# A Fourier filter layer with a two-layer network behind it: other load times in the opening, other PSUM banks for two pieces, and another order of the turned array

## The chip, the cores and the metric

The kernel runs on one core of one Trainium2 chip. A core has a tensor engine (PE, with weight loads shown as PEld), a vector engine (DVE), a scalar engine (ACT), GpSimd (POOL) and SyncE (SP); here POOL and SP mostly issue DMAs, which 16 DMA engines carry out. The metric is the device time of one execution in microseconds (us). The kernel before takes 773.05 us, the median of three runs (772.27 to 773.88).

## What is computed

Eight sequences of 3008 tokens with 256 channels are filtered in the frequency domain, and each token then goes through a two-layer network with a PReLU:

```python
X = np.fft.rfft(x, axis=1)                    # x: (8, 3008, 256)
Y = X * (filt_r + 1j * filt_i)[None]          # (1505, 256)
y = np.fft.irfft(Y, n=3008, axis=1).reshape(24064, 256)
h = y @ w_in                                  # (256, 2048)
g = np.maximum(h, 0) + alpha * np.minimum(h, 0)
out = g @ w_out                               # (2048, 256)
```

## The kernel before

**The whole.** The transform of length 3008 = 94 x 32 is made by matmuls: a first stage over 94 (piece_a), a second over 32 (piece_b) with the product with the filter, the inverse second stage (piece_c), and the inverse first stage (half_d, pair_d), whose result yT has the channels on the partitions and is kept in fp16. The network takes yT in blocks of 512 (or 384) tokens: `up` multiplies by w_in, ACT copies PSUM to gtb, DVE applies the slope, `down` multiplies by w_out, ACT copies out, SP stores. The schedule is written by hand: a plan says at which of 768 steps of the network each piece of the later sequences' transforms is issued, so that PE always has network matmuls to do. Each engine runs its own instructions in program order and waits on semaphores for the others.

**The opening.** The first sequence (class `First`) has nothing to hide behind, so its transform is written out by hand, with matmuls on an identity (`warm`, L438) that keep PE running where it would wait:

- Eight pieces of the first stage (L328), fed by eight DMAs of x from POOL. Piece i writes two PSUM banks (f = 0, 1) and is evicted into `am` (a view of gtb) by ACT or DVE in turn; for pieces 6 and 7 ACT takes f = 0 and DVE f = 1.
- The forward table twf comes in three DMAs from SP (L417), 8 of 24 columns each. The second and third are held back by a small DVE memset of their target (L445 behind piece 3, L453 behind piece 5). From each part PE and ACT make a part of the inverse table (`inverse_table`, L421), and `swapped` (L428, L429) makes from it, by scalings on DVE (part 0) or POOL (parts 8 and 16), a second table twx with swapped signs.
- The filter comes in three groups of eight DMAs from POOL (L140). The second half of the last group is issued behind the scalings of part 8.
- `turn_at` (L343) turns `am` by matmuls with the identity into `at`; `piece_b` (L355) multiplies by the table; DVE multiplies by the filter (L360); `piece_c` (L382) makes the inverse second stage from `uu` with the tables twi and twx as moving operands, into two `op` banks for two successive pieces; `keep_c` evicts these into `vm` (the tile v). There are twelve piece_b and twelve piece_c, kp = 0 to 11.
- `turn` (L399) turns `vm` back, 96 columns at a time, into zt: 32 values of s, two halves f of the channels, so 64 loads of weights. `half_t` does two s in one bank, `piece_t` four in two banks; piece_t(4) to piece_t(7) stand in the plan at steps 19 to 34.
- `half_d` multiplies zt by the inverse table wi3. half_d(0) (channels 0 to 127) and half_d(2) (channels 128 to 255) each need s = 0 to 3, that is half_t(0) and half_t(1).
- The first block goes through `up4` (L569): for each of four columns blocks h the two halves kt of the channels one after the other.

Within `vm` a value stands at (g, q, k, e), where s = 4g + e, q is one of four rows of the inverse table (parity and real or imaginary) and k one of 24 frequencies. So the 96 columns of one s that L399 loads are 4 elements (8 bytes) apart. L382 reads its table for that as

```python
tw, tx = (t.rearrange("p k (c g e) -> p k g c e", c=2, e=4) for t in (twi_s, twx_s))
```

which is runs of four elements, and writes runs of eight. The rows of wi3 have the order (q, k), as in the other sequences.

SP issues the constants that are needed later (wi3, al16, id32, wf1, wfq; L471 to L477) behind the tables. POOL loads the weights w_in and w_out and the next x (L484 to L491) in the loop over kp, behind a DVE memset of win_s (L482) at kp = 4.

Of the kernel before, what the change touches and what calls it, by code (L numbers as in the profile page):

```python
# [14 lines left out]
N1 = 94  # L15
# [10 lines left out]
def _build_consts():  # L26

    n1, n2, p = np.arange(N1), np.arange(N2), np.arange(32)
    k1 = (2 * (np.arange(NK) // 2) + 24 * (np.arange(NK) % 2))[None, :] + np.arange(2)[:, None]
    k2 = np.where(p < 16, p, 47 - p)  # L30
    g = np.where(p < 16, 1.0, -1.0)

    a1 = 2 * np.pi * n1[:, None, None] * k1[None] / N1
    wf1 = np.stack([np.cos(a1), -np.sin(a1)], axis=2)
    scale = np.where((k1 == 0) | (k1 == 47), 1.0, 2.0)[None, :, None, :] / NFFT
    wi3 = (wf1 * scale).reshape(N1, 96).T
    wfx = wf1.transpose(0, 3, 1, 2).reshape(N1, 96)
    wfq = np.zeros((2, 64, 64))
    wfq[:, :47, :48] = wf1[:47].transpose(1, 0, 2, 3).reshape(2, 47, 48)
    wfq = wfq.reshape(128, 64)  # L40
    wf1 = wf1.reshape(N1, 96)

    kk = k1[:, :, None] + N1 * k2
    ang = 2 * np.pi * n2[:, None, None, None] * kk[None] / NFFT
    c, s = np.cos(ang), np.sin(ang)
    fwd = np.array([[c, -s * g], [s, c * g]])
    twf = fwd.transpose(3, 0, 2, 4, 1, 5).reshape(128, NK, 64)
    return wf1, wfx, wfq, wi3, twf


@with_exitstack
def kernel(
# [8 lines left out]
    out: bass.AP,  # L61
):
    nc = tc.nc
    names = ("wf1", "wfx", "wfq", "wi3", "twf")
    consts = {n: nc.inline_tensor(np.ascontiguousarray(v).astype(np.float16), name="c_" + n)
              for n, v in zip(names, _build_consts())}
    signs = [np.tile(np.repeat([1.0, -1.0], r), 64 // r) for r in (16, 32)]
# [19 lines left out]
    wfq_s = konst.tile([128, 64], FP16, name="wfq_s")  # L87
    wfx_s = konst.tile([N1, 96], FP16, name="wfx_s")
    wi3_s = konst.tile([96, N1], FP16, name="wi3_s")
    twf_s = konst.tile([128, NK, 64], FP16, name="twf_s")  # L90
    twi_s = konst.tile([128, NK, 64], FP16, name="twi_s")
    filt_s = konst.tile([128, 12, 2, D], FP16, name="filt_s")
# [66 lines left out]
    class Fft:  # L159
        def __init__(self, b):  # L160
            self.b = b
            self.base = (b % 2) * NFFT
            self.uw = {}

        def start_a(self):
# [114 lines left out]
        def inverse(self, pd, g, dh, mh):  # L280
            ps = pd[:, 0 : 4 * N1].rearrange("p (m x) -> p m x", m=4)
            for m in range(4):
                nc.tensor.matmul(ps[:, m], self.zt[:, 8 * g + 4 * mh + m, dh * 128 : dh * 128 + 128],  # L283
                                 wi3_s, start=True, stop=True)
            return ps

        def half_d(self, i, evict, kind, fill=0):
# [25 lines left out]
    class First(Fft):  # L313
# [7 lines left out]

        def piece_a(self, i, wide):
            c, sh = i // 2, i % 2
            ps = banks(wide)
            for f in range(2):
                for u in range(4):
                    o = (4 * sh + u) * D + 128 * f
                    nc.tensor.matmul(ps[:, f, 96 * u : 96 * u + 96], xc[(0, c)][0:N1, o : o + 128], wfx_s,  # L328
                                     start=True, stop=True)
            o = self.am.rearrange("p (f m s) -> p f m s", f=2, s=N2)[:, :, :, 4 * i : 4 * i + 4]  # L330
            s = ps[:, :, 0:384].rearrange("p f (s m) -> p f m s", s=4)
            if i < 6:
                both[i % 2](o, s)
            else:
                for f in range(2):
                    both[f](o[:, f], s[:, f])

        def turn_at(self, kp, n, evict, wide=False):
            ps = banks(wide)
# [23 lines left out]
        def piece_c(self, kp):  # L363
            if kp % 2 == 0 and kp < 10:
                self.ops = [psO.tile([128, 2, D], FP32, name="op") for _ in range(2)]
            if kp == 10:
                pf = banks(False)
                self.ops = [pf[:, e].rearrange("p (k d) -> p k d", k=2) for e in range(2)]
            if kp == 11:
                pf = [bank(kind) for kind in ("h", "o")]  # L370
                self.ops = [t.rearrange("p (k d) -> p k d", k=2) for t in pf]
            kb = 0 if kp > 9 else kp % 2
            u = self.uw.pop(kp)
            tw, tx = (t.rearrange("p k (c g e) -> p k g c e", c=2, e=4) for t in (twi_s, twx_s))
            for par in range(2):
                for f in range(2):
                    for i, t in enumerate((tw, tx)):
                        for e in range(2):
                            r = slice(64 * e, 64 * e + 64)
                            o = self.ops[e][:, kb].rearrange("p (g w) -> p g w", g=16)  # L380
                            o = o[:, 8 * f : 8 * f + 8, 8 * par : 8 * par + 8]
                            nc.tensor.matmul(o.rearrange("p g (c e) -> p g c e", c=2),  # L382
                                             u[r, par, i, 128 * f : 128 * f + 128], t[r, 2 * kp + par],
                                             start=(i == 0), stop=(i == 1))

        def keep_c(self, kp, evicts, n=2):
            vm = self.vm.rearrange("p (g q k e) -> p g q k e", q=4, k=NK, e=4)
            for e in range(2):
                k = 2 * kp + e
                evicts[e](vm[:, :, :, k : k + 2 * n - 1 : 2],  # L390
                          self.ops[e][:, 0:n].rearrange("p k (g q e) -> p g q k e", q=4, e=4))

        def turn(self, pt, i, n):
            m = self.vm.rearrange("p (g m e) -> p g m e", m=96, e=4)
            for u in range(n):
                for f in range(2):
                    o = 256 * (u % 2) + 128 * f
                    s = n * i + u
                    nc.tensor.matmul(pt[0:96, u // 2, o : o + 128], m[:, 8 * f + s // 4, :, s % 4], id16,  # L399
                                     start=True, stop=True)  # L400

        def half_t(self, i, kind):
            pt = bank(kind).unsqueeze(1)
# [12 lines left out]
    def table(ka, kb):  # L416
        nc.sync.dma_start(out=twf_s[:, ka:kb], in_=consts["twf"].ap()[:, ka:kb])  # L417
# [24 lines left out]
    for i in range(8):  # L442
        f0.piece_a(i, i % 3 < 2)
        if i == 3:
            nc.vector.memset(twf_s[:, 8:16, 0:1], 0.0)  # L445
            table(8, 16)
            inverse_table(0, bank("o"))
            swapped(0, nc.vector)
            warm(3, bank("o"))
        elif i % 2 == 1:  # L450
            warm((8, 0, 6, 0)[i // 2], bank("o"))
        if i == 5:
            nc.vector.memset(twf_s[:, 16:24, 0:1], 0.0)  # L453
            table(16, 24)
    load_filt(nc.gpsimd, filt_s, 4, 8)
    warm(5, bank("o"))
    f0.turn_at(0, 1, on_act)
# [2 lines left out]
    f0.piece_b(0)  # L460
    f0.turn_at(2, 2, on_act)
    inverse_table(8, bank("o"))
    load_filt(nc.gpsimd, filt_s, 8, 12, (0,))
    swapped(8, nc.gpsimd)
    load_filt(nc.gpsimd, filt_s, 8, 12, (1,))
    f0.piece_b(1)
    inverse_table(16, bank("o"))
    swapped(16, nc.gpsimd)
    f0.piece_b(2)
    f0.turn_at(4, 2, on_act)  # L470
    nc.sync.dma_start(out=wi3_s, in_=consts["wi3"].ap())  # L471
# [4 lines left out]
    for r in (slice(0, 64), slice(64, 128)):  # L476
        nc.sync.dma_start(out=wfq_s[r], in_=consts["wfq"].ap()[r])  # L477
    for kp in range(12):
        if 0 < kp < 10:
            f0.piece_b(kp + 2)  # L480
        if kp == 4:
            nc.vector.memset(win_s[:, :, 0:1], 0.0)  # L482
            for kt in range(2):
                nc.gpsimd.dma_start(out=win_s[:, kt], in_=moe_w_in[kt * 128 : (kt + 1) * 128])  # L484
            xc[(1, 0)] = load_x(1, 0)
            for q in range(2):
                nc.gpsimd.dma_start(
                    out=wout_s[:, 8 * q : 8 * q + 8],
                    in_=moe_w_out[1024 * q : 1024 * q + 1024].rearrange("(j p) d -> p j d", p=128))
            for c in range(1, 4):  # L490
                xc[(1, c)] = load_x(1, c)  # L491
# [12 lines left out]
    for o in (32, 96):  # L504
        nc.gpsimd.dma_start(out=filt_s[o : o + 32], in_=filt_s[o - 32 : o])
    warm(3, bank("h"))
    on_dve(*f0.half_t(0, "o"))
    on_act(*f0.half_t(1, "o"))
    later = [f0.half_t(2, "h"), f0.half_t(3, "f")]
    f0.half_d(0, on_act, "o")  # L510
    f0.half_d(2, on_dve, "o")

    sizes = [512] * 5 + [384] + [512] * 6
    blocks = []
# [21 lines left out]
    class Block:  # L536
# [26 lines left out]
        def up4(self, i, half, mid):  # L563
            ps = psH.tile([128, 2, 512], FP32, name="hps").rearrange("p b (q c) -> p (b q) c", q=2)
            t = slice(256 * half, 256 * half + 256)
            for h in range(4):
                j = 4 * i + h
                for kt in range(2):
                    nc.tensor.matmul(ps[:, h], win_s[:, kt, j * 128 : (j + 1) * 128], yT[:, kt, t],  # L569
                                     start=(kt == 0), stop=(kt == 1))  # L570
            for fn in mid:
                fn()
            if half == 0:
# [190 lines left out]
```

## Time and profile before

| what | value |
|---|---|
| median of three runs | 773.05 us (772.27 to 773.88) |
| the profiled execution | 772.3 us, span 770.5 us, granted clock 1.0 |
| PE busy | 760.9 us, 99% of the span |
| weight loads (PEld) busy | 510.2 us, 66% |
| DVE busy | 634.2 us, 82% |
| ACT busy | 583.2 us, 76% |
| POOL busy | 147.9 us, 19% |
| 64 weight loads of L399 | 182 ns mean |
| 192 matmuls of L382 | 186 to 200 ns each, overlapping |
| 12 multiplications of L360 | 1215 ns each |

The span is the time from the first to the last record of the profiled execution; the execution's own time is 1.8 us longer. Matmuls overlap in the record, so the distance from one start to the next says more than a duration. In the timeline and the chain a row is start, time, engine, line, operation, out<-in, and behind a bracket the idle time before it with what ended it. A line with L is a line of the kernel before, except where the changed kernel is named.

### The profile page before, as it was taken

Reading aid. Unit: us, or ns where it says so; the run is one execution under the profiler, and the core shown is the slowest. Engines: PE = TensorE matmul, PEld = TensorE weight load, DVE = VectorE, ACT = ScalarE, POOL = GpSimd, SP = SyncE. Lnnn points to the kernel's source line nnn. Section 1 sums busy time; section 2 is a strip of 40 time slices with the busy share of each in tenths; the row PEclk is TensorE's granted clock in tenths of the full one; section 3 lists DMA queues with packets and bytes.
Section 4 is the critical chain, followed back from the end, with each engine's and each line's share of the span. In section 5 each row is a group of like instructions: output and inputs, shape, how many; then the busy total and the mean of one; then the engine's idle time right before and its main releaser. Section 6 shows DMA issues by size and latency. Waiting matters only on the chain.

```text
span 770.5 us, 16598 instructions
## 1 busy us (share of the span) xinstructions
PE 760.9 (99%) x6550; PEld 510.2 (66%) x6550; DVE 634.2 (82%) x1160; ACT 583.2 (76%) x671; POOL 147.9 (19%) x278
## 2 busy tenths in 40 slices
PE   8999999999999999999999999999999999999998
PEld 4666657666666666666666666766666666766666
DVE  4888885889889998899988998999877888666663
ACT  4787788888778787887778777787767777776663
POOL 7620560132211212121201222022101212000000
PEclk9999999999999999999999999999999999999999
DMA  9995797664954558633883538644473223510111
GB/s 162 148 239 156 134 208 195 171 164 119 200 138 94 138 126 169 185 83 94 188 213 89 124 98 177 182 99 117 119 160 98 68 72 96 152 36 28 42 42 56
DMA packets 96814, 99.77 MB, mean 129 GB/s; under 512 B 12020, under 2 KB 83076, under 8 KB 96544
## 3 DMA queue, kind: packets, MB, share of 16 engines
q1 hardware_dynamic: 82048, 69.22, 32.7%
q0 software_dynamic: 14688, 29.49, 21.4%
q8 instruction: 51, 0.84, 0.5%
q14 instruction: 27, 0.22, 0.1%
HBM read 54.74 MB, written 46.66 MB: 132 GB/s over the span
## 4 chain that ended last, share of the span: by engine, by line
PE 96%; ACT 3%; issue 0%; DVE 0%; DMA 0%; ACTq 0%
PE op L600 42%; PE hps L546 41%; PE psF L283 3%; PE hps L261 2%; PE psF L230 1%; PE hps L176 1%; PE op L438 1%; PE hps L202 1%; ACT asb L305 1%; PE hps L569 1%; ACT v L305 1%; PE op L382 1%; PE psF L399 0%; ACT gtb L577 0%; ACT gtb L555 0%; PE hps L355 0%
## 5 line engine op out<-in xcount | busy, mean ns | idle before, releaser
L555 ACT ACTIVATE gtb<-hps 128x1024 f16<-128x1024 f32 (+1 forms) x376 | 377.4, 1006 | 134.7 <-PE hps L546 131.6
L600 PE MATMUL op<-wout_s,gtb 128*128 128x256 f16 x3008 | 431.4, 273 | 0.0
L546 PE MATMUL hps<-yT,win_s 128*128 128x512 f16 (+1 forms) x1504 | 418.4, 375 | 0.9 <-ACT asb L305 0.5
L600 PEld LDWEIGHTS <-gtb 128*128 128x128 f16 x3008 | 290.8, 98 | 164.5 <-issue 11.0
L558 DVE TENSOR_SCALAR m<-gtb,alm_s 128x512 f16<-128x512 f16 (+1 forms) x752 | 227.2, 346 | 98.4 <-ACT gtb L555 96.9
L560 DVE TENSOR_TENSOR gtb<-gtb,m 128x2048 f16<-128x2048 f16 (+1 forms) x188 | 226.1, 1203 | 10.7 <-DVE m L558 0.5
L546 PEld LDWEIGHTS <-win_s 128*128 128x128 f16 x1504 | 142.5, 98 | 55.2 <-issue 6.6
L244 POOL DMA_DIRECT2D sw<-ww x144 | 71.6, 505 | 414.6 <-DVE ww L237 408.8
L605 ACT ACTIVATE osb<-op 128x512 f32<-128x512 f32 (+1 forms) x97 | 56.6, 584 | 12.6 <-PE op L600 11.5
L305 ACT ACTIVATE asb<-hps 128x1024 f16<-128x1024 f32 (+1 forms) x56 | 56.6, 1020 | 5.6 <-PE hps L176 4.3
L305 ACT ACTIVATE v<-hps 128x1024 f16<-128x1024 f32 (+1 forms) x43 | 43.4, 1010 | 10.8 <-PE hps L261 10.6
L237 DVE TENSOR_TENSOR ww<-psF,filts_s 128x1024 f16<-128x1024 f32 x42 | 51.1, 1218 | 0.2 <-PE psF L230 0.2
L238 DVE TENSOR_TENSOR uu<-psF,filt_s 128x1024 f16<-128x1024 f32 x42 | 51.0, 1214 | 0.0
L305 ACT ACTIVATE yT<-psF 128x752 f16<-128x752 f32 x58 | 46.1, 796 | 2.0 <-PE psF L283 1.9
L283 PEld LDWEIGHTS <-zt 96*128 96x128 f16 x512 | 28.6, 98 | 6.3 <-issue 0.6
L283 PE MATMUL psF<-wi_s,zt 96*128 96x94 f16 x496 | 31.0, 205 | 0.3 <-DVE yT L308 0.2
L249 DVE TENSOR_TENSOR uu<-uu,sw 128x1024 f16<-128x1024 f16 x36 | 24.6, 683 | 1.7 <-DMA sw<-ww 1.3
L242 POOL DMA_DIRECT2D uu<-ww x24 | 19.5, 1238 | 33.0 <-DVE uu L238 24.9
L118 POOL DMA_DIRECT2D xs<-in_x_dram x32 | 21.6, 889 | 13.0 <-PE hps L546 4.9
L186 DVE TENSOR_TENSOR xs<-xs 47x2048 f16<-47x2048 f16 x16 | 19.5, 1220 | 0.4
L190 DVE TENSOR_TENSOR xs<-xs 47x2048 f16<-47x2048 f16 x16 | 19.3, 1209 | 0.0
L261 PE MATMUL hps<-uu,twi_s 64*64 64x256 f16 x336 | 17.3, 281 | 0.0
(86 smaller groups left out, 264.2 us busy)
## 6 DMA issues: line engine op xcount, KB each, us to landing
out_dram<-osb SPq DMA_DIRECT2D x128, 128.0 KB
v_dram<-v SPq DMA_DIRECT2D x84, 128.0 KB
zt<-v_dram SPq DMA_DIRECT2D x28, 384.0 KB
sw<-ww POOLq DMA_DIRECT2D x144, 64.0 KB, 2.8
xs<-in_x_dram POOLq DMA_DIRECT2D x44, 192.0 KB, 6.3
at<-a_dram SPq DMA_DIRECT2D x40, 192.0 KB
a_dram<-asb SPq DMA_DIRECT2D x32, 192.0 KB
a_dram<-asb SPq DMA_DIRECT2D x12, 384.0 KB
```

The lines of the kernel that those rows point to most:

```text
L237: nc.vector.tensor_mul(ww, px, fs)
L238: nc.vector.tensor_mul(uu, px, f)
L244: nc.gpsimd.dma_start(out=sw[o : o + 32], in_=ww[i : i + 32])
L261: nc.tensor.matmul(ps[64 * par : 64 * par + 64, e, 256 * h : 256 * h + 256], twi_s[r, 4 * q + 2 * h + par], u[r, par, h], start=True, stop ...
L283: nc.tensor.matmul(ps[:, m], self.zt[:, 8 * g + 4 * mh + m, dh * 128 : dh * 128 + 128], wi3_s, start=True, stop=True)
L305: nc.scalar.activation(o, i, AF.Copy)
L546: nc.tensor.matmul(self.hps[:, j % 2, 0:tn], win_s[:, kt, j * 128 : (j + 1) * 128], yT[:, kt, self.t0 : self.t0 + tn], start=(kt == 0), st ...
L555: nc.scalar.activation(g[:, 2 * i : 2 * i + 2], self.hps[:, :, 0:tn], AF.Copy)
L558: nc.vector.tensor_scalar(m[:, 2 * i + h], g[:, 2 * i + h], 0.0, a, OP.min, OP.mult)
L560: nc.vector.tensor_add(g, g, m)
L600: nc.tensor.matmul(self.op[:, si - s0], self.gts[k][:, 128 * si : 128 * si + 128], wout_s[:, k], start=(si == s0 and k == 0), stop=(si == ...
L605: nc.scalar.activation(osb[:, 0:m], self.op[:, 0:m], AF.Copy)
```

## The change

1. The second and third part of the forward table are loaded behind pieces 5 and 7, not 3 and 5.
2. Pieces 6 and 7 of the first stage take two separate banks each (piece 6 two `op`, piece 7 two `hps`), so that each engine evicts a tile of its own.
3. The last group of filter DMAs is issued whole, ahead of the scalings of part 8; the memset of win_s, and with it the loads of weights, moves from kp = 4 to kp = 3.
4. `vm` stands in the order (s, k, q). The 96 columns of an s are adjacent; L382 reads single elements of its table from two places in turn, 64 bytes apart, and writes runs of two, with the loops over f and par exchanged. The rows of the inverse table for the first sequence now have the order (k, q), which needs a table of its own, wif; wfq is loaded by one DMA in place of two.
5. The first two turns are done by halves of the channels (`side_t`), ACT and DVE exchange their evictions there, and up4 does all four h for kt = 0 and then for kt = 1.

```diff
+    wif = (wf1 * scale).transpose(3, 1, 2, 0).reshape(96, N1)
...
+            self.wi = wi3_s if b else wif_s
...
-            ps = banks(wide)
+            if i < 6:
+                ps = banks(wide)
+                pf = [ps[:, f] for f in range(2)]
+            else:
+                pf = [bank("oh"[i - 6]) for f in range(2)]
...
-            tw, tx = (t.rearrange("p k (c g e) -> p k g c e", c=2, e=4) for t in (twi_s, twx_s))
-            for par in range(2):
-                for f in range(2):
+            tw, tx = (t.rearrange("p k (c s) -> p k s c", c=2) for t in (twi_s, twx_s))
+            for f in range(2):
+                for par in range(2):
                     for i, t in enumerate((tw, tx)):
                         for e in range(2):
                             r = slice(64 * e, 64 * e + 64)
-                            o = self.ops[e][:, kb].rearrange("p (g w) -> p g w", g=16)
-                            o = o[:, 8 * f : 8 * f + 8, 8 * par : 8 * par + 8]
-                            nc.tensor.matmul(o.rearrange("p g (c e) -> p g c e", c=2),
+                            o = self.ops[e][:, kb].rearrange("p (s q) -> p s q", q=4)
+                            nc.tensor.matmul(o[:, 32 * f : 32 * f + 32, 2 * par : 2 * par + 2],
                                              u[r, par, i, 128 * f : 128 * f + 128], t[r, 2 * kp + par],
                                              start=(i == 0), stop=(i == 1))
...
-            vm = self.vm.rearrange("p (g q k e) -> p g q k e", q=4, k=NK, e=4)
+            vm = self.vm.rearrange("p (s k q) -> p s k q", q=4, k=NK)
...
-                    nc.tensor.matmul(pt[0:96, u // 2, o : o + 128], m[:, 8 * f + s // 4, :, s % 4], id16,
+                    nc.tensor.matmul(pt[0:96, u // 2, o : o + 128], m[:, f, n * i + u], id16,
                                      start=True, stop=True)
+
+        def side_t(self, f):
+            pt = bank("o")
+            for u in range(4):
+                nc.tensor.matmul(pt[0:96, 128 * u : 128 * u + 128],
+                                 self.vm.rearrange("p (f s m) -> p f s m", f=2, m=96)[:, f, u], id16,
+                                 start=True, stop=True)
+            return self.zt[:, 0:4, 128 * f : 128 * f + 128], pt[0:96].rearrange("p (s d) -> p s d", s=4)
...
         if i == 3:
-            nc.vector.memset(twf_s[:, 8:16, 0:1], 0.0)
-            table(8, 16)
             inverse_table(0, bank("o"))
...
-        if i == 5:
-            nc.vector.memset(twf_s[:, 16:24, 0:1], 0.0)
-            table(16, 24)
+        if i in (5, 7):
+            ka = 4 * i - 12
+            nc.vector.memset(twf_s[:, ka : ka + 8, 0:1], 0.0)
+            table(ka, ka + 8)
...
-    load_filt(nc.gpsimd, filt_s, 8, 12, (0,))
+    load_filt(nc.gpsimd, filt_s, 8, 12)
     swapped(8, nc.gpsimd)
-    load_filt(nc.gpsimd, filt_s, 8, 12, (1,))
...
-        if kp == 4:
+        if kp == 3:
             nc.vector.memset(win_s[:, :, 0:1], 0.0)
...
-    on_dve(*f0.half_t(0, "o"))
-    on_act(*f0.half_t(1, "o"))
+    on_act(*f0.side_t(0))
+    on_dve(*f0.side_t(1))
     later = [f0.half_t(2, "h"), f0.half_t(3, "f")]
-    f0.half_d(0, on_act, "o")
-    f0.half_d(2, on_dve, "o")
+    f0.half_d(0, on_dve, "o")
+    f0.half_d(2, on_act, "o")
...
-            for h in range(4):
-                j = 4 * i + h
-                for kt in range(2):
+            for kt in range(2):
+                for h in range(4):
+                    j = 4 * i + h
                     nc.tensor.matmul(ps[:, h], win_s[:, kt, j * 128 : (j + 1) * 128], yT[:, kt, t],
-                                     start=(kt == 0), stop=(kt == 1))
+                                     start=(kt == 0 and h % 2 == 0), stop=(kt == 1 and h % 2 == 1))
```

More of the change, by code (lines that the diff above doesn't have):

```diff
@@ L47, in _build_consts @@
     twf = fwd.transpose(3, 0, 2, 4, 1, 5).reshape(128, NK, 64)
-    return wf1, wfx, wfq, wi3, twf
+    return wf1, wfx, wfq, wi3, wif, twf
 @with_exitstack
@@ L63 @@
     nc = tc.nc
-    names = ("wf1", "wfx", "wfq", "wi3", "twf")
+    names = ("wf1", "wfx", "wfq", "wi3", "wif", "twf")
     consts = {n: nc.inline_tensor(np.ascontiguousarray(v).astype(np.float16), name="c_" + n)
@@ L89 @@
     wi3_s = konst.tile([96, N1], FP16, name="wi3_s")
+    wif_s = konst.tile([96, N1], FP16, name="wif_s")
     twf_s = konst.tile([128, NK, 64], FP16, name="twf_s")
@@ L283, in inverse @@
                 nc.tensor.matmul(ps[:, m], self.zt[:, 8 * g + 4 * mh + m, dh * 128 : dh * 128 + 128],
-                                 wi3_s, start=True, stop=True)
+                                 self.wi, start=True, stop=True)
             return ps
@@ L327, in piece_a @@
                     o = (4 * sh + u) * D + 128 * f
-                    nc.tensor.matmul(ps[:, f, 96 * u : 96 * u + 96], xc[(0, c)][0:N1, o : o + 128], wfx_s,
+                    nc.tensor.matmul(pf[f][:, 96 * u : 96 * u + 96], xc[(0, c)][0:N1, o : o + 128], wfx_s,
                                      start=True, stop=True)
             o = self.am.rearrange("p (f m s) -> p f m s", f=2, s=N2)[:, :, :, 4 * i : 4 * i + 4]
-            s = ps[:, :, 0:384].rearrange("p f (s m) -> p f m s", s=4)
             if i < 6:
-                both[i % 2](o, s)
+                both[i % 2](o, ps[:, :, 0:384].rearrange("p f (s m) -> p f m s", s=4))
             else:
                 for f in range(2):
-                    both[f](o[:, f], s[:, f])
+                    both[f](o[:, f], pf[f][:, 0:384].rearrange("p (s m) -> p m s", s=4))
         def turn_at(self, kp, n, evict, wide=False):
@@ L386, in keep_c @@
         def keep_c(self, kp, evicts, n=2):
-            vm = self.vm.rearrange("p (g q k e) -> p g q k e", q=4, k=NK, e=4)
+            vm = self.vm.rearrange("p (s k q) -> p s k q", q=4, k=NK)
             for e in range(2):
                 k = 2 * kp + e
-                evicts[e](vm[:, :, :, k : k + 2 * n - 1 : 2],
-                          self.ops[e][:, 0:n].rearrange("p k (g q e) -> p g q k e", q=4, e=4))
+                evicts[e](vm[:, :, k : k + 2 * n - 1 : 2],
+                          self.ops[e][:, 0:n].rearrange("p k (s q) -> p s k q", q=4))
         def turn(self, pt, i, n):
-            m = self.vm.rearrange("p (g m e) -> p g m e", m=96, e=4)
+            m = self.vm.rearrange("p (f s m) -> p f s m", f=2, m=96)
             for u in range(n):
@@ L397, in turn @@
                     o = 256 * (u % 2) + 128 * f
-                    s = n * i + u
-                    nc.tensor.matmul(pt[0:96, u // 2, o : o + 128], m[:, 8 * f + s // 4, :, s % 4], id16,
+                    nc.tensor.matmul(pt[0:96, u // 2, o : o + 128], m[:, f, n * i + u], id16,
                                      start=True, stop=True)
+        def side_t(self, f):
[5 more added lines that the diff above has]
+            return self.zt[:, 0:4, 128 * f : 128 * f + 128], pt[0:96].rearrange("p (s d) -> p s d", s=4)
         def half_t(self, i, kind):
@@ L470 @@
     f0.turn_at(4, 2, on_act)
-    nc.sync.dma_start(out=wi3_s, in_=consts["wi3"].ap())
+    nc.sync.dma_start(out=wif_s, in_=consts["wif"].ap())
     nc.sync.dma_start(out=al16, in_=moe_alpha.rearrange("(j p) -> j p", p=128))
@@ L475 @@
         nc.sync.dma_start(out=wf1_s[r], in_=consts["wf1"].ap()[r])
-    for r in (slice(0, 64), slice(64, 128)):
-        nc.sync.dma_start(out=wfq_s[r], in_=consts["wfq"].ap()[r])
+    nc.sync.dma_start(out=wfq_s, in_=consts["wfq"].ap())
+    nc.sync.dma_start(out=wi3_s, in_=consts["wi3"].ap())
     for kp in range(12):
```

## The prediction

> **What bounds the kernel now.** I read the page's busy shares first, then the busy time by stretch, then the chain of waits over the first 48 us, and last the timeline and the groups by form at the lines that the change touches.
>
> ```profile
> PE 760.9 (99%) x6550; PEld 510.2 (66%) x6550; DVE 634.2 (82%) x1160; ACT 583.2 (76%) x671; POOL 147.9 (19%) x278
> ...
> PE 96%; ACT 3%; issue 0%; DVE 0%; DMA 0%; ACTq 0%
> ```
>
> The tensor engine (PE) is the bound. The view by stretch says where it is not full:
>
> ```profile
> 0.00:16.84 16.84, 14.19 (x134) 8.01 (x135) 5.32 (x11) 5.67 (x8) 12.01 (x27) 1.00 0.90 164
> 16.84:30.70 13.86, 12.64 (x400) 7.86 (x397) 13.78 (x13) 11.06 (x17) 12.53 (x21) 1.00 0.82 118
> 30.70:46.00 15.30, 14.29 (x155) 11.65 (x154) 10.32 (x19) 10.70 (x16) 4.11 (x8) 1.00 1.22 216
> 46.00:770.50 724.50, 719.74 (x5870) 482.69 (x5867) 604.76 (x1118) 555.75 (x632) 119.30 (x222) 1.00 0.52 127
> ```
>
> The columns are the stretch, its length, then the busy time of PE, weight loads, DVE, ACT and POOL, the granted clock (1.00), the DMA share and GB/s. After 46 us PE is busy 719.7 of 724.5 us, so whatever the first batch's opening gains or loses arrives at the end unchanged, and in the later part only PE work counts. All edits but one half lie before 46 us. In the opening the chain of waits runs like this:
>
> ```profile
> 13.08 0.36 PE hps L328 x8
> 13.44 0.02 issue
> 13.46 0.50 ACT gtb L305
> 13.96 0.02 issue
> 13.98 1.03 DVE gtb L308 x2
> 15.01 0.05 issue
> 15.06 0.34 PE psF L343 x3
> ...
> 17.09 1.03 ACT at L305
> 18.12 0.04 issue
> 18.16 0.41 PE hps L355 x16
> 18.57 0.55 PE psF L343 x8
> ```
>
> From there to 30 us it is a ping-pong: two ACT evictions (1.08), piece_c (0.39), piece_b (0.34), piece_c (0.39), 2.24 us for each pair of pieces. DVE's L360 (1.131 from start to start, 2.26 a pair) runs beside it and is just as full. Then the turn L399 and its evictions lead to the first up4 at 34.20.
>
> **The change, part by part** (minus is gain; line numbers are those of the kernel before).
>
> *Own banks for pieces 6 and 7.* ACT and DVE shared one tile; DVE began at 13.98, when ACT's first eviction had ended. With own banks DVE waits only for piece 6's matmuls. The eight matmuls (42 ns apart from 12.92, 0.2 to drain) end by 13.44, so its two evictions (0.557 and 0.547, 0.48 apart) end at 14.46, not 15.00. The turn L343 could then start at once; it is held by warm(5), after which its first matmul stood at 14.68 already. Its second goes from 15.06 to 14.74: **-0.32 us**.
>
> *Tables two pieces later.* SyncE issued the two later parts at 11.29 and 12.85, behind the memsets; by the trace's semaphore records they landed at 15.01 and 16.55, both 3.70 to 3.72 after issue, while the first part, in a nearly empty queue, took 2.59 (1.50 to 4.09). Now the first goes at 12.85 and lands by 16.55; L421 for it stood at 16.83 and moves to 16.5: no loss. The second waits behind DVE's last eviction and memset (14.46), so it is issued at 14.5. Its reader L421 stood at 17.54 and moves to 17.22. At 3.7 it lands at 18.2, and PE, in order, stops there for 1.0 us with piece_b(2), the next turn and piece_c(0) behind it. Of this 0.38 falls in the time that PE waited for ACT until 18.16 anyway: L421 at 18.25, four matmuls 0.22, piece_b(2) at 18.47 in place of 18.16, **+0.31 in place of -0.32**. At 2.59 it lands at 17.1 and nothing stops. I take 3.7, because the DMA engines are 0.90 and 0.82 busy in these stretches; the bounds are -0.32 and +0.31, and another 0.3 if it is later still. The small constants queued behind on SP (wif, needed at 33; wf1, at 45) have over 10 us, and their number is the same (wif added, wfq whole). The filter landing that held L360 to 16.84 may come sooner; it gates DVE, not this chain: nothing.
>
> The Trainium skill ("DMA: Bandwidth & Descriptors", section "Anatomy of one DMA — SWDGE (gpsimd) path") fits a DMA as 2.0 us plus bytes over 436 GB/s, 2.3 us for these 128 KB, though for the other path. By it the part lands at 16.8 and there is no stop; the trace's 3.7 speaks against it under this load.
>
> *Scalings behind the filter loads.* POOL issues the four last filter DMAs (2.1 us) first, at 19.54 in place of 21.01, and swapped(8) (0.94 + 0.48) ends at about 23.2 in place of 21.06. Its first reader is piece_c(4), whose second matmul ran at 23.62 and will run at 23.9: covered by 0.7, and still by 0.1 if the table stop is not there. The four DMAs must each wait for the landing eight issues before (18.67 to 20.29 by the semaphore records), which is earlier than their new issue times. The win_s memset a piece earlier lets POOL issue win_s at 24.6, not 25.18; its second half landed at 34.04 and the first up4 needs it now at 34.2 minus gains: covered by the same 0.6. Sum 0.
>
> *The turned array contiguous.* It has a gain and an unknown price. The gain:
>
> ```profile
> L399 PEld LDWEIGHTS <-v 128*96 128x96 f16 x64 | 6.5, 182 | 0.7 <-ACT v L305 0.4
> ...
> L176 PEld LDWEIGHTS <-wf_s 94*96 94x96 f16 x48 | 5.5, 124 | 0.8 <-issue 0.5
> ...
> L343 PEld LDWEIGHTS <-gtb 128*128 128x128 f16 x48 | 2.8, 97 | 1.2 <-DVE gtb L308 0.5 <-issue 0.4
> ```
>
> Busy and mean ns stand behind the bar. L399 loads 96 columns eight bytes apart, 182 ns; L176 loads 96 adjacent ones, 124. In the timeline L399's loads follow each other every 90 ns, L343's pairs with the same 128-column matmul every 56. With 58 ns less per load I take 56 for L399 too: 34 ns on each of 64. The 32 in the main loop are PE work on the chain: **-1.09**. The 32 in the opening are in the next part. The unknown: piece_c (L382), with the same 16 loads and matmuls in another order of loops, now reads its moving table one element at a time from two places 64 bytes apart, where it read runs of four, and writes runs of two, where it wrote eight. Before, two matmuls on two row halves go every 29.2 ns, 64 columns at the 0.43 ns that L343 takes per column (56 over 128): the present gaps cost nothing. Lower bound: nothing again, and no less, since PE is at that rate already. By the strided weight load, 90 ns for 96 columns, it is 0.94 ns a column, 60 ns a pair, +31 x 8 pairs x 12 pieces = +3.0, all in the ping-pong. Counted by jumps, L399 makes 48 (two columns to 16 bytes), 1.88 ns each; 64 jumps are 120 ns, +91 x 96 = +8.7. ACT's eviction at L305 (yT, 128x752, 796 ns) reads every element from another place and costs no more per element than the 128x1024 rows (1006 ns). I take **0**, the present rate of this very row, and keep both ends for the range.
>
> *side_t, the swapped evictions, up4 by kt.* Now 16 turns take 31.79 to 34.20 to reach the first up4. After: side_t(0) is in PSUM at 32.16 (4 x 56 ns and 0.2), ACT evicts to 32.77 (0.59), half_d(0) is done at 33.15, DVE (free at 33.09) evicts it by 33.72 (0.55), and up4's first four matmuls start at 33.77; the other four follow 0.44 later, when ACT's yT (33.97) is there. Eight at 109 ns end at 34.64, where they ended at 35.20: **-0.56**. The next eight turns (piece_t at 35.95) give 0.25, of which DVE, evicting behind them, passes on 0.17: **-0.17**. half_t(6) and (7) hide behind DVE: 0.
>
> **Sum**: +0.31 - 0.56 - 0.17 - 1.09 = -1.51 us. The profiled execution took 772.3 (span 770.5 and 1.8 around it), 0.75 under the median 773.05; from the median the forecast is **771.5**.
>
> **The rivals.**
> 1. *The table is in time* (2.6 to 2.8 us): -0.32 for +0.31, -2.14, **770.9**. For it: fewer packets queue when the other part has gone. Against it: even small constants issued at 13.2 to 16.2 took 3.5 to 3.9.
> 2. *L382 reads at the strided rate of the weights*: -1.5 + 3.0, **774.5**. For it: L399 against L176, the same engine reading the same memory. Against it: runs of four cost nothing.
> 3. *Each jump has its price* (slower): -1.5 + 8.7, **780.2**. Each piece_c then takes 0.73 us more, and both of a pair of pieces stand in the ping-pong on PE; the loss decides from 16 ns per pair of matmuls on (1.51 over 96), where the other gains are used up. The Trainium skill ("Advanced Engine Details and Errata", section "Memory Cachelines") speaks for 2 or 3: an SBUF line of 16 bytes should be hit twice in a row, and a new line at each access is penalised; it gives no price. By it L399's two columns per line should be free, which 182 against 124 ns contradicts, and its warning that any gap in a PSUM access slows matmuls is not borne out by 29.2 ns for the present gaps.
> 4. *Adjacent weights are no faster*, the change not doing what it says: L399 stays at 90 ns, the 1.09, the 0.17 and some 0.3 of the 0.56 go, **773.1**.
>
> **How the numbers follow.** Forecast 0.40, rivals 0.16, 0.20, 0.18, 0.06. About 0.2% (1.5 us, 771.5 to 774.6) is what a measurement of this kernel can tell from no change. The forecast lies on that bound: 0.22 of it faster, 0.18 same. Rival 1 faster 0.15, same 0.01; rival 2 half and half; 3 slower; 4 same. That is faster 0.37, same 0.35, slower 0.28. The range runs from 770.2 (rival 1 with a quicker filter) to 777.5, between rivals 2 and 3, and leaves out most of rival 3 and a little below. The forecast's own range is 770.5 to 772.6.
>
> **What would show it.** DVE's first 128x384 eviction at 13.5, not behind ACT; L421's third group waiting for the table to about 18.2; L382's pairs 29 ns apart (rival 2: 60, rival 3: 120); L399's loads at 124 ns and 56 apart; the first up4 about 0.1 before its old time. The forecast is wrong if L382's spacing has grown.

## The result and the profile after

The changed kernel takes 775.62 us (median of nine runs, 774.86 to 776.43) against 773.11 us for the kernel before: a ratio of 1.003 with a 95% interval of 1.002 to 1.004. It is slower by 0.3%, where the forecast was 771.5, faster by 0.2%. The time lies in the forecast's range, near its second rival (774.5). The profiled execution took 775.22 us with a span of 773.4, 2.9 us more than the 770.5 of before.

The page of the changed kernel, busy shares and the chain's shares, shows the same bound as before:

```profile
PE 763.1 (99%) x6550; PEld 510.8 (66%) x6550; DVE 634.3 (82%) x1160; ACT 583.4 (75%) x671; POOL 148.2 (19%) x278
...
PE 94%; DVE 3%; ACT 2%; DMA 1%; issue 0%; ACTq 0%
```

The view by stretch, with the same borders as before (the first stretch, 14.29 us of PE, is left out), tells where the 2.9 us came from:

```profile
16.84:30.70 13.86, 12.27 (x339) 8.11 (x337) 12.52 (x12) 10.23 (x15) 12.25 (x21) 1.00 0.84 128
30.70:46.00 15.30, 14.68 (x198) 10.56 (x198) 9.15 (x14) 8.61 (x14) 4.07 (x8) 0.89 1.22 213
46.00:773.40 727.40, 721.88 (x5891) 483.90 (x5888) 607.12 (x1124) 558.86 (x635) 119.54 (x222) 1.00 0.50 127
```

From 16.84 to 30.70 PE is nearly as busy as before (12.27 against 12.64 us), and 339 matmuls lie in the stretch where 400 did: part of the second stage now comes later, and its matmuls take longer. From 30.70 to 46 us the granted clock is 0.89, where it was 1.00. The chain of waits of the changed kernel in the opening:

```profile
13.68 1.02 DVE gtb L311 x2
...
14.78 3.51 DMA twf_s<-c_twf
...
18.33 0.40 PE op L433 x4
18.73 0.34 PE hps L361 x16
...
22.33 0.65 PE op L387 x15
22.98 0.34 PE hps L361 x16
23.32 0.64 PE op L387 x16
23.96 1.08 ACT v L308 x2
```

L433, L361, L387 and L308 are the L421, L355, L382 and L305 of before. Three things are to be seen. The table's last part is now in the chain: issued at 14.78, landed 3.51 us later at 18.28 (forecast: issued at 14.5, 3.7 us, 18.2). The ping-pong that follows still has ACT's two evictions (1.08) and piece_b (0.34), but each piece_c takes 0.65 us where it took 0.39, so a pair of pieces takes 2.76 in place of 2.24. And the group of the turn's weight loads did get faster, as forecast:

```profile
L403 PEld LDWEIGHTS <-v 128*96 128x96 f16 x56 | 3.9, 123 | 0.5
```

That is 123 ns for 182. In the matmul records they follow each other every 56 ns.

I compared the two traces matmul by matmul (the nth PE matmul of the one against the nth of the other, minus is earlier than before). The differences are +0.18 at 10 us, where no edit has acted yet; +0.49 at piece_b(2); +2.40 halfway through the ping-pong; +4.17 behind the last piece_c; +3.33 when the opening's turns are done; +2.91 from 69 us on, and +2.89 at the last matmul. The experiments take this row apart; each is compared with the kernel before in the same way. "By the matmuls" below means this comparison.

### The profile page after: what moved, and what is told of

Read it like the earlier page. It is cut to its first block, busy times and chain, and to the rows that moved or that the text cites. A ratio compares the mean times of both kernels' runs of the same rounds, so it can differ in the third digit from the quotient of the medians.

```text
span 773.4 us, 16598 instructions
## 1 busy us (share of the span) xinstructions
PE 763.1 (99%) x6550; PEld 510.8 (66%) x6550; DVE 634.3 (82%) x1160; ACT 583.4 (75%) x671; POOL 148.2 (19%) x278
## 4 chain that ended last, share of the span: by engine, by line
PE 94%; DVE 3%; ACT 2%; DMA 1%; issue 0%; ACTq 0%
PE op L610 42%; PE hps L556 41%; PE psF L286 3%; PE hps L264 2%; PE psF L233 1%; PE op L450 1%; PE hps L179 1%; PE hps L205 1%; PE op L387 1%; DVE gtb L593 1%; DVE zt L311 1%; ACT asb L308 1%; DVE m L592 1%; ACT v L308 1%; DMA twf_s<-c_twf 0%; ACT gtb L565 0%
## 5 line engine op out<-in xcount | busy, mean ns | idle before, releaser
L308 ACT ACTIVATE asb<-hps 128x1024 f16<-128x1024 f32 (+1 forms) x56 | 56.6, 1019 | 5.6 <-PE hps L179 4.3
L308 ACT ACTIVATE v<-hps 128x1024 f16<-128x1024 f32 (+1 forms) x43 | 43.4, 1010 | 10.8 <-PE hps L264 10.6
L308 ACT ACTIVATE yT<-psF 128x752 f16<-128x752 f32 x58 | 46.1, 795 | 2.0 <-PE psF L286 1.9
L286 PEld LDWEIGHTS <-zt 96*128 96x128 f16 x512 | 28.5, 98 | 7.2 <-issue 1.2
L286 PE MATMUL psF<-wi_s,zt 96*128 96x94 f16 x448 | 27.9, 205 | 0.1
```

What stands on the lines that cost most here:

```text
L308: nc.scalar.activation(o, i, AF.Copy)
```

## The experiments

Theory: L382's new way through its operands costs 30 ns a pair of matmuls and more than eats what the adjacent weights give; the table's stop adds a little. Rivals: the loss is the late table's, or that of the clock, which fell to a half for a stretch.

**1. All but the turned array.** The array v, L382, the turns and the inverse table's order as before; the rest is the changed kernel. Of the edit the line of keep_c:

```diff
-            vm = self.vm.rearrange("p (s k q) -> p s k q", q=4, k=NK)
+            vm = self.vm.rearrange("p (g q k e) -> p g q k e", q=4, k=NK, e=4)
```

> The changed kernel with the turned array in its old order (columns 8 bytes apart, table read in runs of four), all else as changed. Theory A (single-element reads in L382 are the cost, +0.26 us a piece, and they thin PE's work so much that the granted clock halves for 3.4 us): L382 back at 29 ns a pair, L399's loads back at 90 ns apart, clock full throughout, total within 0.5 us of the kernel before, since the table stop (+0.5 us) and the gain of the halved turns (-0.4 us) remain. Theory B (the late table is the main cost, the reads do little): stays 1.5 to 2.5 us slower than before.

Measured: 772.85 us, ratio 0.9997 (0.9988 to 1.0006), no difference. By the matmuls L382's pairs are 28 to 30 ns apart again. The chain of this kernel, at the same place:

```profile
14.94 3.99 DMA twf_s<-c_twf
...
18.97 0.40 PE op L435 x4
```

Here the part needs 3.99 us, the stop is there, piece_b(2) stands 1.14 late (0.35 of it from the start of the run), and 0.94 of this is still there at the end. So the loss of the changed kernel hangs on the array.

**2. The array alone.** The kernel before with v in the new order, L382 to match, and the inverse table for it with its loads; nothing else. Of the edit the line that reads the table:

```diff
-            tw, tx = (t.rearrange("p k (c g e) -> p k g c e", c=2, e=4) for t in (twi_s, twx_s))
+            tw, tx = (t.rearrange("p k (c s) -> p k s c", c=2) for t in (twi_s, twx_s))
```

> The kernel before with the new order of the turned array alone (and the table wif that it needs). Theory A: L382 at 62 ns a pair, L399's loads 56 ns apart, no table stop; 2.0 us slower than before if the clock stays full, 3.0 if it halves again. Theory B: no slower than before, about -1 us from the 64 faster loads.

Measured: 774.72 us, ratio 1.0024 (1.0015 to 1.0033). The pairs are 61 to 64 ns apart from start to start; by the matmuls +0.04 at piece_b(2), +3.70 behind the last piece_c, +3.06 when the opening's turns are done, +2.67 at the end. The array alone makes the kernel slower, without a stop at the table. In this profile too the clock fell to a half, for 3.41 us.

**3. Tables as early as before.** The changed kernel with the second and third part of the table loaded behind pieces 3 and 5.

```diff
+            nc.vector.memset(twf_s[:, 8:16, 0:1], 0.0)
+            table(8, 16)
...
-        if i in (5, 7):
-            ka = 4 * i - 12
+        if i == 5:
+            ka = 16
```

> The changed kernel with the two later table parts loaded behind pieces 3 and 5 as before. Theory A: only the stop at L421 goes, 0.5 us less than the changed kernel (2.0 us over before); if the clock's halving needed the stop as well, 1.3 us less. Theory B: 2 us or more less, about equal to before.

Measured: 774.10 us, ratio 1.0016 (1.0007 to 1.0025). The clock stayed full in this profile, so it gives L382's price alone: +0.07 at piece_b(2), +2.93 behind the last piece_c, which is **+2.86 us** for twelve pieces. Experiment 2 with the half clock lost 3.66 on the same way, the changed kernel 3.68; **the half clock is thus worth 0.82 us** in these two profiles. Within one kernel it is less: by the mean clock (0.997 or 0.998) it fell in 5 of the 11 runs of experiment 2 and in 4 of the 11 of experiment 3, and the median of these is 0.6 us above that of the others (775.11 and 774.53; 774.58 and 773.99).

The +0.07 at piece_b(2) hides something. Up to the last part's L433 PE stands 0.45 early in this run, and 0.52 is lost there:

```profile
13.67 3.28 DMA filt_s<-in_filt_r_dram
...
16.96 1.24 DVE uu L366
...
18.24 0.41 PE hps L361 x16
```

DVE waits for the first filter parts, and piece_b(2) for DVE's first product. The forecast had put this landing at nothing ("it gates DVE, not this chain").

**4. Runs of four read, single elements written.** The changed kernel, but L382 reads runs of four from its table, as before, and writes single fp32 values 16 bytes apart. The order of the output is the same.

```diff
-            tw, tx = (t.rearrange("p k (c s) -> p k s c", c=2) for t in (twi_s, twx_s))
+            tw, tx = (t.rearrange("p k (c g e) -> p k g c e", c=2, e=4) for t in (twi_s, twx_s))
...
-                            o = self.ops[e][:, kb].rearrange("p (s q) -> p s q", q=4)
-                            nc.tensor.matmul(o[:, 32 * f : 32 * f + 32, 2 * par : 2 * par + 2],
+                            o = self.ops[e][:, kb].rearrange("p (g e q) -> p g q e", e=4, q=4)
+                            nc.tensor.matmul(o[:, 8 * f : 8 * f + 8, 2 * par : 2 * par + 2],
```

> The changed kernel, but L382 reads its tables in runs of four as before and writes its results singly, 16 bytes apart, to the same places, so that the turned array stays contiguous. Theory A (reads): L382 back at 29 ns a pair, clock full, total 0.7 us under the kernel before (table stop +0.5, halved turns -0.4, adjacent loads -0.8). Theory C (the gaps in the PSUM writes cost, not the reads): L382 stays at 62 ns or is slower, total as the changed kernel or worse.

Measured: 774.27 us, ratio 1.0017 (1.0008 to 1.0026); the pairs are 55 to 56 ns apart, a piece 0.60 us. So reading in runs isn't enough: single writes are nearly as dear. The clock stayed full in this profile, and by the mean clock in 10 of the 11 runs; the table's stop is in this one (+1.02 at piece_b(2)).

**5. The turn put into the eviction.** If both ends of L382 must stay as before, v can still be made contiguous by keep_c: ACT and DVE read PSUM in the other order instead. Tables as in experiment 3, L382 as before. Of the edit the lines of keep_c's eviction:

```diff
-                evicts[e](vm[:, :, k : k + 2 * n - 1 : 2],
-                          self.ops[e][:, 0:n].rearrange("p k (s q) -> p s k q", q=4))
+                evicts[e](vm[:, k : k + 2 * n - 1 : 2],
+                          self.ops[e][:, 0:n].rearrange("p k (g q e) -> p k g e q", q=4, e=4))
```

> The changed kernel with the tables early again, L382 reading runs of four and writing runs of eight as before, and the new contiguous order of the turned array made by the eviction of keep_c, which reads PSUM permuted. Theory A (both gaps, single-element reads and single writes, slow L382; the eviction's order is free): L382 at 29 ns a pair, evictions at 0.55 us each, L399's loads 56 apart, no table stop, clock full: 1.5 us under the kernel before (-0.4 turns, -0.3 banks, -0.8 loads). Rival: the eviction pays for the gaps, 0.25 us or more longer each, and the total is no better than before.

Measured: **771.34 us, ratio 0.997 (0.9959 to 0.9981)**, faster than both kernels. The chain of this kernel, in the ping-pong and then in the first blocks of the network:

```profile
24.07 0.39 PE op L388 x15
...
25.19 1.08 ACT v L308 x2
...
52.66 1.13 DVE zt L311
53.79 0.53 DVE m L571 x2
...
54.34 1.22 DVE gtb L573
...
56.12 1.14 DVE zt L311
...
57.30 0.49 PE psF L286 x8
```

ACT's eviction in another order costs what it did (1.08 for two). By the matmuls the twelve piece_c cost nothing more here (+0.52 at piece_b(2), +0.44 behind the last). Of the +0.52, 0.42 arise at piece_b(2) itself, where PE waits 0.64 us for DVE's first product. That starts at 17.40, and by the trace's semaphore records the last of the eight filter parts that it needs landed at 17.28.

The later rows answer a question of the forecast, where the gain of the main loop went: between 48 and 57 us it is DVE, not PE, that is followed back, through its slopes and its two evictions of zt, and L286 waits for it. By the matmuls the two turns at 49 and 54 us gain 0.47 together, and at L286 all of it is given back; the two turns at 65 and 67 us gain 0.43, and that stays. The changed kernel has the same steps: DVE's last zt from 59.80, L286 at 60.98. In the kernel before the chain goes through PE at this place, but DVE was not behind it by anything. In its timeline the second zt ends at 57.60, and the matmuls that read it start 0.05 later, as soon as PE comes to them:

```profile
56.39 1.21 DVE L308 CAST zt<-psF 96x1024 f16<-96x1024 f32 x1
57.65 0.49 PE L283 MATMUL psF<-wi_s,zt 96*128 96x94 f16 x8
```

**6. How short may a run be?** Experiment 5 with runs of two read and runs of four written:

```diff
-            tw, tx = (t.rearrange("p k (c g e) -> p k g c e", c=2, e=4) for t in (twi_s, twx_s))
+            tw, tx = (t.rearrange("p k (c g e) -> p k g c e", c=2, e=2) for t in (twi_s, twx_s))
...
-                            o = o[:, 8 * f : 8 * f + 8, 8 * par : 8 * par + 8]
+                            o = o[:, 16 * f : 16 * f + 16, 4 * par : 4 * par + 4]
...
```

> As the run before, but with reads in runs of two elements and writes in runs of four. If the price is that of a lone element (an engine that takes two neighbours at once), L382 stays at 29 ns a pair and the total as there. If it is a price for each jump, the 32 jumps cost half of what 64 do: 40 to 50 ns a pair and about +1.2 us.

And experiment 3 with single elements read, as in the changed kernel, and 64 adjacent values written, so that only the reads are broken; the evictions have half the size and twice the number.

```diff
-                            o = self.ops[e][:, kb].rearrange("p (s q) -> p s q", q=4)
-                            nc.tensor.matmul(o[:, 32 * f : 32 * f + 32, 2 * par : 2 * par + 2],
+                            o = self.ops[e][:, kb].rearrange("p (q f s c) -> p q f s c", q=2, f=2, c=2)
+                            nc.tensor.matmul(o[:, par, f],
...
```

> The changed kernel with early tables, L382 reading single elements as in the change but writing 64 adjacent results; the eviction reorders, in twice as many instructions, so that the total says little. If reads alone make the change's 62 ns a pair, it stays at 58 to 65. If the writes made it, 29. If both add, in between.

Measured: 771.58 us, ratio 0.9983 (0.9974 to 0.9993), for the first; one run of 774.15 us for the second. The groups of L382's form by 17 to 36 us in five kernels, one line each, busy and mean ns behind the bar: before; reads of two; single reads with adjacent writes; reads of four with single writes; the changed kernel.

```profile
L382 PE MATMUL op<-gtb,uu 64*128 64x64 f16 x84 | 4.1, 189 | 0.0
```

```profile
L388 PE MATMUL op<-gtb,uu 64*128 64x64 f16 x84 | 4.7, 197 | 0.0
```

```profile
L387 PE MATMUL op<-gtb,uu 64*128 64x64 f16 x84 | 6.8, 221 | 0.0
```

```profile
L387 PE MATMUL op<-gtb,uu 64*128 64x64 f16 x84 | 6.5, 242 | 0.0
```

```profile
L387 PE MATMUL op<-gtb,uu 64*128 64x64 f16 x84 | 6.7, 221 | 0.0
```

Single durations overlap, so the busy time says more than the mean. Reads of two, with writes of four, cost 0.05 us a piece (0.44 for 0.39; the pairs mostly 35 to 38 ns apart), singles 0.26. The third and the last line are alike: with the writes adjacent, the single reads alone make the changed kernel's whole price, and its writes in runs of two add nothing to it. Whether runs of two would cost by themselves with reads of four wasn't tried. The Trainium skill ("Advanced Engine Details and Errata", section "Memory Cachelines") says that a line of 16 bytes in SBUF should be hit at least twice in a row, and that in PSUM every two consecutive elements should be contiguous; both rules agree with these pieces (two in a row 0.44, one 0.60 to 0.65). The same section's sentence that any gap in a PSUM access slows matmuls significantly doesn't: runs of eight and of four run at 0.39 and 0.44. And its rule for SBUF does not hold for weights, where two columns to a line took 182 ns against 123.

**7. Identity matmuls against the clock.** The changed kernel with `warm(2)` behind piece_c(7) also.

```diff
-        if 7 < kp < 10:
+        if 6 < kp < 10:
```

> The changed kernel with two more identity matmuls (warm) behind piece_c(7), where PE now waits 0.8 us for ACT. Theory A (PE's thinner work halves the granted clock for 3.4 us): the clock stays full and the time is 0.5 to 0.9 us less than the changed kernel's. Rival (the halving has another reason or costs nothing): halved again, or no less time.

Measured: 775.10 us, ratio 1.0022 (1.0013 to 1.0031). The stretch in which the changed kernel's clock fell, first in that kernel (28.08 to 31.50 is the 3.41 us before), then around the same time in this one; the granted clock is the number ahead of the last two:

```profile
28.08:31.50 3.42, 2.81 (x80) 1.75 (x74) 3.15 (x3) 1.72 (x3) 2.51 (x5) 1.00 1.05 202
31.50:34.91 3.41, 3.35 (x62) 1.64 (x61) 1.22 (x1) 1.14 (x3) 0.87 (x3) 0.50 1.13 197
```

```profile
30.60:35.40 4.80, 4.62 (x103) 2.78 (x103) 2.84 (x4) 2.41 (x7) 1.24 (x4) 1.00 1.10 205
```

The clock stays full here, and by the mean clock in 9 of 12 runs, against 1 of 9 of the changed kernel and 72 of 85 of the kernel before. In time little of it is left: in this profile the table's last part took 3.94 us, and the intervals of the two kernels overlap. The counts speak for an effect on the clock; a gain of 0.82 us in the median is not shown.

**8. The banks alone.** Experiment 1 with the tables as early as before: own banks, the scalings' place and the changes of the turns' order are left.

```diff
+            nc.vector.memset(twf_s[:, 8:16, 0:1], 0.0)
+            table(8, 16)
...
-        if i in (5, 7):
-            ka = 4 * i - 12
+        if i == 5:
+            ka = 16
```

> The changed kernel with the array v in its old order and the table's later parts loaded where they were: what is left is the own banks of the last first-stage pieces and the scalings behind the filter loads. Theory: the stop at L421 of 0.4 to 1.1 us that the changed kernel and the kernel with v apart show at piece_b(2) goes, the own banks keep 0.3 to 0.4 us (piece_b(2) 0.3 us before its old time), and this stays to the end: median 772.5, 0.3 to 0.4 us under the kernel before, and last matmul 0.3 earlier in its trace. Rival: the own banks' gain is covered by the next wait (a table part or an eviction), piece_b(2) at its old time and 773.0.

Measured: 772.29 us, ratio 0.9986 (0.9977 to 0.9995); in this profile PE starts 0.39 early, and by the matmuls it stands at -0.50 at piece_b(2), -0.10 at 24 us and -0.24 at the end. The banks are worth 0.11 (from -0.39 to -0.50), not 0.3. At 24 us the chain of this kernel shows what comes next:

```profile
21.40 0.54 POOL filt_s L142
...
22.07 0.96 POOL gtb L442
23.02 0.47 POOL gtb L443
...
23.53 0.38 PE op L388 x14
```

The scalings, now behind the four filter DMAs, end at 23.49, and piece_c(4) waits for them: 0.4 us lost by an edit that is free as long as PE comes later.

**9 and 10. The late tables on the faster kernel.** Experiment 5 with both later parts loaded as late as in the changed kernel, and with only the last part late.

```diff
-            nc.vector.memset(twf_s[:, 8:16, 0:1], 0.0)
-            table(8, 16)
...
-        if i == 5:
-            ka = 16
+        if i in (5, 7):
+            ka = 4 * i - 12
```

> The kernel that turns v in its eviction (771.3), with the table's parts loaded as late as in the changed kernel. Theory: the last part lands at 18.3 to 19.0, piece_b(2) stands 0.5 to 1.1 us later than with the early parts, and PE carries it to the end: 772.0 to 772.4, still under the kernel before, and nothing is halved in the clock because the second stage is as dense as before. Rival: the later stages have 0.5 us of slack that takes it up (DVE's wait at 57 us is a fixed time), 771.3 to 771.6.

```diff
-        if i == 5:
+        if i == 7:
             ka = 16
```

> The same kernel, of the table's later parts only the last (16 to 24) moved behind piece_a(7), the other as before. Theory: the last part's landing alone makes the stop, so the time is that of the kernel with both parts late, 772.0 to 772.4. Rival: the middle part (8 to 16) makes it, or the two slow each other, and the time stays at 771.3.

Measured: 772.07 us, ratio 0.998 (0.997 to 0.999), and 772.41 us, ratio 0.9992 (0.9982 to 1.0001). Both lie over the 771.34 of experiment 5, and in both the chain goes through the last part (14.82 to 18.65, and 14.08 to 18.07). Moving that part is enough to make the stop; it costs 0.7 to 1.1 us between medians; the interval of the first overlaps that of experiment 5, that of the second just does not. By the matmuls, each less the start of its run, the two stand about 0.4 and 0.6 us behind experiment 5 at the end.

## Why the prediction was wrong, point by point

The step that failed is the price of L382: "I take **0**, the present rate of this very row". It measured +2.86 us. The terms, in us, against the changed kernel's trace:

| step | forecast | measured | from |
|---|---|---|---|
| start of the run | - | +0.18 | at 10 us |
| own banks (within the next row) | -0.32 | -0.11 | experiment 8 |
| late table, net | +0.31 | +0.31 | +0.49 less the start |
| scalings | 0 | 0; +0.4 once PE is early | experiment 8 |
| L382 | 0 | +2.86 | experiment 3 |
| granted clock | not foreseen | +0.82 | experiments 2 and 3 |
| opening's turns, side_t, up4 | -0.73 | -0.84 | 4.17 to 3.33 |
| loads in the main loop | -1.09 | -0.43 | 3.33 to 2.90 |
| sum | -1.51 | +2.9 | |

- **L382.** The pairs went to 62 ns, the second rival (60), and its price of +3.0 was right within 0.15. Some of that is luck, since the weights' rate belongs to another pattern: two reads in a row within 16 bytes took the weights 0.94 ns a column (90 over 96), and the moving operand of experiment 6 about 0.56 (36 over 64). The forecast had weighed one row (ACT reading every element from another place at no cost) against another (PE's weights at 90 ns for 56) and took the first. The reader is PE, so PE's row was the nearer one; and ACT's row isn't quite free either (796 ns over 752 elements is 1.06 each, 1006 over 1024 is 0.98). Experiment 4 and the second kernel of experiment 6 show that either end, singly, is enough to lose it.
- **The late table.** Landing (18.28 against 18.2) and net loss are as forecast in this profile, by luck in part: the issue came 0.28 later than forecast, the part took 0.19 less. In others the part took 3.8 to 4.05 us and the net loss was 0.6 to 0.9, at the outer bound (0.31 and "another 0.3 if it is later still") or over it.
- **Own banks.** DVE started at 13.68, not at 13.98, as forecast, but the gain didn't follow. The turn is led by the identity matmuls of warm(5), and these write an `op` bank that is now piece 6's. In experiment 5 they start at 14.04, just after ACT's eviction of such a bank has ended (13.49 + 0.49), with 0.23 us between them and the matmul before, where 0.04 is the rule. That this eviction holds them is read from these times; the list of waits doesn't name it.
- **Scalings.** The cover was named ("still by 0.1 if the table stop is not there") and was thinner than that. In the changed kernel the stop hides it.
- **The filter landing.** It was put at nothing and is not. In the kernel before, piece_b(2)'s weights waited for DVE's product until 18.12, next to ACT's eviction until 18.16. In experiments 3 and 5, with the tables early, the same wait cost PE 0.52 and 0.42 us. In the changed kernel the table's stop hides it.
- **Opening's turns.** The sum is nearly right, 0.84 for 0.73, the parts are not: to the end of the first up4 0.50 for 0.56, from there on 0.34 for 0.17. Most comes from the faster loads (0.64 in experiment 2, without side_t and the new up4); side_t and up4 alone gain 0.11 in experiment 1.
- **Main loop.** The first load of each turn of eight gains nothing (55 ns to the next in both kernels); the others gain 29 to 36 ns. By the matmuls that is 0.24 a turn and 0.95 for the 32, where 34 each made 1.09. Half of it, 0.47, lies ahead of a wait for DVE at L286 and is lost. PE's 99% of the span, and the chain of the kernel before, had hidden that DVE was level with PE there, so that a faster PE only meets DVE's wait.
- **The clock.** Nothing in the profile of before pointed at it. It fell in 13 of 85 runs of the kernel before, in 4 and 5 of 11 with the single reads and the tables early, and in 8 of 9 of the changed kernel, which has the table's stop as well; with the stop and without the single reads (experiment 1) in none of 11. That the slower L382 makes it more likely is what these counts say; how it does so is open.

The cause of the loss is settled in its main part: L382's reads, +2.86. With them comes the half clock in eight of nine runs (+0.82 between profiles, 0.6 between runs of one kernel); the gains are 1.27. Experiment 5 shows that they exist when nothing is taken from L382: 771.34.

## What to carry to other kernels

An order of elements that is free for one engine need not be so for another: price a new access pattern by a row of the engine that makes it, and let the engine that evicts anyway do the turning (ACT's read in another order cost nothing here, PE's 0.26 us a piece). A share of 99% over the span doesn't say how far the next engine is behind, and neither does the chain, which names only the last one: at the place in which a gain is claimed, measure the time between the end of the other engine's work and the start of what reads it (0.05 us here, for a claimed 0.54). Every cover that a step leans on should be checked for the case that the other steps succeed: the scalings were hidden only by the stop that another edit made.

## What the runs showed of the hardware

- Moving operands: sixteen matmuls in pairs, of 64 columns each, took 0.39, 0.44 and 0.65 us with fp16 reads in runs of four, two and one; with reads of four and single fp32 writes 16 bytes apart 0.60.
- In the profiles of the changed kernel and of experiment 2 the granted clock falls for one stretch of 3.41 us, with PE busy in 2.81 of the 3.42 us before and idle in 0.61 us in all. The Trainium skill ("TensorE: Matmul & The Clock Gate", section "Part 1: The HAM clock gate (the "warmup" mystery)") describes windows of 3.4 us that run freely and a half clock after an idle one. The length agrees (3.413 us), the idle window doesn't: 82% of it were busy. The share alone doesn't decide, since experiment 10's kernel was busy in only 2.28 us of the 3.41 from 15.47 on, 0.67, and kept its clock; what decides stays open.
- The table's parts of 128 KB landed in 3.5 to 4.05 us at this load, whether one or two of them were late.
